# A windowed attention stage traced in a fixed order of TensorE instructions, with PSUM copies moved from VectorE to ScalarE

## The chip, the core and the metric

The kernel runs on one core of one Trainium2 chip. The metric is the device time of one execution in microseconds. A profile is one execution taken by the hardware profiler; its span runs from the first to the last instruction. Engines are named PE (TensorE matmul), PEld (TensorE weight load), DVE (VectorE), ACT (ScalarE), POOL (GpSimd) and SP (SyncE); a q after the name (SPq, ACTq) is the engine's queue of DMA issues.

## The reference

Attention with a causal window of 64 positions, then a gated feed-forward block. There are 8 batches and 8 heads, 576 positions, a head size of 64; the feed-forward block has 4608 tokens of 512 values and an inner size of 1536.

```python
scores = scale * np.matmul(q, k.transpose(0, 1, 3, 2))
mask = (rel >= 0) & (rel < window)          # window = 64, rel = row - column
scores = np.where(mask, scores, -1000000000.0)
... # softmax over the last axis
attn_out = np.matmul(attn, v)
x = attn_out.transpose(0, 2, 1, 3).reshape(B * S, H * D)
g = x @ w_gate
out = (g / (1 + np.exp(-g))) * (x @ w_val) @ w_out
```

## The kernel before

The kernel has two stages. The attention stage treats the 64 pairs of batch and head one after the other and fills xT, the attention's result with features on partitions, in bf16 in SBUF. The feed-forward stage then reads xT in nine tiles of 512 tokens. The change touches the attention stage alone.

A head is cut into nine blocks of 64 rows. Each block needs two blocks of keys (128 of them), and the blocks are worked in two groups, eight and one. The steps for a head, in the kernel's own words:

```python
nat = ...tile_pool(name="nat", bufs=2)      # q, k, v as loaded, and q_bf, k_bf
tp_pool = ...tile_pool(name="tps", bufs=2)  # qT, kT, v_aug, vs_aug
grp = ...tile_pool(name="grp", bufs=2)      # E, R, Dm, OU_sb
psA = ...(name="psA", bufs=2, space=PSUM)   # S_ps, OU, XT
psB = ...(name="psB", bufs=1, space=PSUM)   # tpq, tpk

# loads: q and v on SyncE's queue, k and the shifted v on ScalarE's
nc.sync.dma_start(q_nat[:, 0:4, :], ...)
nc.sync.dma_start(q_nat[0:64, 4, :], ...)
nc.scalar.dma_start(k_nat[:, 0:4, :], ...)
nc.scalar.dma_start(k_nat[0:64, 4, :], ...)
nc.sync.dma_start(v_nat[:, 0:4, :], ...)
nc.scalar.dma_start(vs_nat[:, :, :], ...)
# casts to bf16, then transposes through PSUM
nc.vector.tensor_copy(q_bf..., q_nat...)    # two, and two for k
for c in range(4):
    nc.tensor.transpose(tpq[:, 128*c:128*c+128], q_bf[:, c, :], identb[:])
    nc.tensor.transpose(tpk[:, 128*c:128*c+128], k_bf[:, c, :], identb[:])
nc.tensor.transpose(tpq[:, 512:576], ...)
nc.tensor.transpose(tpk[:, 512:576], ...)
nc.scalar.copy(qT[:, :], tpq[:, 0:576])
nc.vector.tensor_copy(kT[:, :], tpk[:, 0:576])
# v with a column of ones, so that OU's last column is the softmax sum
nc.vector.memset(...); nc.vector.memset(...)
nc.vector.tensor_copy(v_aug..., v_nat...); nc.vector.tensor_copy(vs_aug..., vs_nat...)
for gi, blocks in enumerate([list(range(8)), [8]]):
    for mu, i in enumerate(blocks):
        nc.tensor.matmul(S_ps[:, mu, :], kT[:, k0:k0+128], qT[:, 64*i:64*i+64])
    nc.scalar.activation(E, S_ps, AF.Exp, bias=0.0, scale=SCALE)
    nc.vector.tensor_mul(E, E, mask_t)
    for mu, i in enumerate(blocks):
        nc.tensor.matmul(OU[tt][:, jj, :], E[:, mu, :], vv)
    nc.vector.reciprocal(R, OU[tt][:, :, 64])            # one for each OU tile
    nc.vector.tensor_mul(Dm, ident8, R.to_broadcast(...))
    nc.vector.tensor_copy(OU_sb, OU[tt][:, :, 0:64])     # one for each OU tile
    for mu, i in enumerate(blocks):
        nc.tensor.matmul(XT[po:po+64, mu, :], OU_sb[:, mu, :], Dm[:, mu, :])
    nc.scalar.copy(xT[po:po+64, kc, ...], XT[po:po+64, ...])
```

The last matmul transposes a block and divides it by its softmax sum in one go: Dm is a diagonal matrix of reciprocals. The order in which the instructions of several heads are mixed on each engine is left to the scheduler. The weights are loaded first, 3 MB each for w_gate and w_out on SyncE's queue and for w_val on ScalarE's, and are cast to bf16 by VectorE.

The feed-forward stage makes, for each of 9 tiles and 12 slices of the inner size, four matmuls into g_ps and four into v_ps, a sigmoid on ScalarE and two products on VectorE; then 48 matmuls into o_ps, whose results go out through ScalarE.

Of the kernel before, what the change touches and what calls it, by code (L numbers as in the profile page):

```python
# [8 lines left out]
P = 128  # L9
FP32 = mybir.dt.float32  # L10
BF16 = mybir.dt.bfloat16
AF = mybir.ActivationFunctionType
# [4 lines left out]
def kernel(  # L17
# [10 lines left out]
    nc = tc.nc  # L28
    B, H, S, D = 8, 8, 576, 64
# [4 lines left out]
    SCALE = 1.0 / 8.0  # L34

    persist = ctx.enter_context(tc.tile_pool(name="persist", bufs=1))
    xT = persist.tile([P, 4, NTOK], BF16, name="xT")
# [14 lines left out]
    identb = persist.tile([P, P], BF16, name="identb")  # L52
    make_identity(nc, identb[:])
    ident8 = persist.tile([64, 8, 64], BF16, name="ident8")
# [22 lines left out]
    mask_reg = persist.tile([P, 8, 64], BF16, name="mask_reg")  # L77
    build_band(mask_reg[:], 8)
    mask_first = persist.tile([P, 8, 64], BF16, name="mask_first")
# [5 lines left out]
        base=0, pattern=[[1, 64]], channel_multiplier=-1,  # L85
    )

    with ExitStack() as actx:
        nat = actx.enter_context(tc.tile_pool(name="nat", bufs=2))
        tp_pool = actx.enter_context(tc.tile_pool(name="tps", bufs=2))  # L90
        grp = actx.enter_context(tc.tile_pool(name="grp", bufs=2))
        psA = actx.enter_context(tc.tile_pool(name="psA", bufs=2, space=bass.MemoryType.PSUM))
        psB = actx.enter_context(tc.tile_pool(name="psB", bufs=1, space=bass.MemoryType.PSUM))

        for b in range(B):
            for h in range(H):
                po = (h % 2) * 64
                kc = h // 2
                qbh = q[b, h]
                kbh = k[b, h]  # L100
                vbh = v[b, h]

                q_nat = nat.tile([P, 5, D], FP32, name="q_nat", tag="q_nat")
                k_nat = nat.tile([P, 5, D], FP32, name="k_nat", tag="k_nat")
                v_nat = nat.tile([P, 4, D], FP32, name="v_nat", tag="v_nat")
                vs_nat = nat.tile([P, 4, D], FP32, name="vs_nat", tag="vs_nat")
                nc.sync.dma_start(q_nat[:, 0:4, :], qbh[0:512].rearrange("(c p) d -> p c d", p=P))
                nc.sync.dma_start(q_nat[0:64, 4, :], qbh[512:576])
                nc.scalar.dma_start(k_nat[:, 0:4, :], kbh[0:512].rearrange("(c p) d -> p c d", p=P))
                nc.scalar.dma_start(k_nat[0:64, 4, :], kbh[512:576])  # L110
                nc.sync.dma_start(v_nat[:, 0:4, :], vbh[0:512].rearrange("(c p) d -> p c d", p=P))
                nc.scalar.dma_start(vs_nat[:, :, :], vbh[64:576].rearrange("(c p) d -> p c d", p=P))

                q_bf = nat.tile([P, 5, D], BF16, name="q_bf", tag="q_bf")
                k_bf = nat.tile([P, 5, D], BF16, name="k_bf", tag="k_bf")
                nc.vector.tensor_copy(q_bf[:, 0:4, :], q_nat[:, 0:4, :])  # L116
                nc.vector.tensor_copy(q_bf[0:64, 4, :], q_nat[0:64, 4, :])
                nc.vector.tensor_copy(k_bf[:, 0:4, :], k_nat[:, 0:4, :])  # L118
                nc.vector.tensor_copy(k_bf[0:64, 4, :], k_nat[0:64, 4, :])
                qT = tp_pool.tile([64, S], BF16, name="qT", tag="qT")  # L120
                kT = tp_pool.tile([64, S], BF16, name="kT", tag="kT")
                tpq = psB.tile([64, 640], BF16, name="tpq", tag="tpq")
                tpk = psB.tile([64, 640], BF16, name="tpk", tag="tpk")
                for c in range(4):
                    nc.tensor.transpose(tpq[:, 128 * c:128 * c + 128], q_bf[:, c, :], identb[:])  # L125
                    nc.tensor.transpose(tpk[:, 128 * c:128 * c + 128], k_bf[:, c, :], identb[:])  # L126
                nc.tensor.transpose(tpq[:, 512:576], q_bf[0:64, 4, :], identb[0:64, 0:64])  # L127
                nc.tensor.transpose(tpk[:, 512:576], k_bf[0:64, 4, :], identb[0:64, 0:64])
                nc.scalar.copy(qT[:, :], tpq[:, 0:576])  # L129
                nc.vector.tensor_copy(kT[:, :], tpk[:, 0:576])  # L130

                v_aug = tp_pool.tile([P, 5, 65], BF16, name="v_aug", tag="v_aug")
                vs_aug = tp_pool.tile([P, 4, 65], BF16, name="vs_aug", tag="vs_aug")
                nc.vector.memset(v_aug[:, :, 64:65], 1.0)
                nc.vector.memset(vs_aug[:, :, 64:65], 1.0)
                nc.vector.tensor_copy(v_aug[:, 0:4, 0:64], v_nat[:, 0:4, :])
                nc.vector.tensor_copy(vs_aug[:, :, 0:64], vs_nat[:, :, :])

                groups = [list(range(8)), [8]]
                for gi, blocks in enumerate(groups):  # L140
                    nb = len(blocks)
                    mask_t = mask_first if (gi == 0) else mask_reg
                    S_ps = psA.tile([P, 8, 64], FP32, name="S_ps", tag="S_ps")
                    for mu, i in enumerate(blocks):
                        k0 = 0 if i == 0 else 64 * (i - 1)
                        nc.tensor.matmul(  # L146
                            S_ps[:, mu, :],
                            kT[:, k0:k0 + 128],
                            qT[:, 64 * i:64 * i + 64],
                        )  # L150
                    E = grp.tile([P, 8, 64], BF16, name="E", tag="E")
                    nc.scalar.activation(  # L152
                        E[:, 0:nb, :], S_ps[:, 0:nb, :], AF.Exp, bias=0.0, scale=SCALE
                    )
                    nc.vector.tensor_mul(E[:, 0:nb, :], E[:, 0:nb, :], mask_t[:, 0:nb, :])  # L155

                    ntiles = 2 if nb == 8 else 1
                    OU = []
                    for tt in range(ntiles):
                        OU.append(psA.tile([64, 4, 65], FP32, name="OU", tag="OU"))  # L160
                    for mu, i in enumerate(blocks):
                        tt = mu // 4
                        jj = mu % 4
                        if i == 0:
                            vv = v_aug[:, 0, :]
                        elif i % 2 == 1:
                            vv = v_aug[:, (i - 1) // 2, :]
                        else:
                            vv = vs_aug[:, (i - 2) // 2, :]
                        nc.tensor.matmul(OU[tt][:, jj, :], E[:, mu, :], vv)  # L170
                    R = grp.tile([64, 8], FP32, name="R", tag="R")
                    for tt in range(ntiles):
                        nbt = min(4, nb - 4 * tt)
                        nc.vector.reciprocal(R[:, 4 * tt:4 * tt + nbt], OU[tt][:, 0:nbt, 64])
                    Dm = grp.tile([64, 8, 64], BF16, name="Dm", tag="Dm")
                    nc.vector.tensor_mul(  # L176
                        Dm[:, 0:nb, :],
                        ident8[:, 0:nb, :],
                        R[:, 0:nb].to_broadcast((64, nb, 64)),
                    )  # L180
                    OU_sb = grp.tile([64, 8, 64], BF16, name="OU_sb", tag="OU_sb")
                    for tt in range(ntiles):
                        nbt = min(4, nb - 4 * tt)
                        nc.vector.tensor_copy(  # L184
                            OU_sb[:, 4 * tt:4 * tt + nbt, :], OU[tt][:, 0:nbt, 0:64]
                        )
                    XT = psA.tile([P, 8, 64], FP32, name="XT", tag="XT")
                    for mu, i in enumerate(blocks):
                        nc.tensor.matmul(  # L189
                            XT[po:po + 64, mu, :],  # L190
                            OU_sb[:, mu, :],
                            Dm[:, mu, :],
                        )
                    i0 = blocks[0]
                    t0 = b * S + 64 * i0
                    nc.scalar.copy(  # L196
                        xT[po:po + 64, kc, t0:t0 + 64 * nb],
                        XT[po:po + 64, 0:nb, :],
                    )

    with ExitStack() as fctx:
        fps = fctx.enter_context(tc.tile_pool(name="fps", bufs=2, space=bass.MemoryType.PSUM))
# [70 lines left out]
```

The softmax here doesn't subtract the row's maximum and nothing guards it: scores larger than these inputs give would overflow.

## Time and profile before

| | |
|---|---|
| time, median of 6 runs | 605.72 us (605.02 to 606.32) |
| span of the profiled run | 604.6 us |
| PE busy | 519.7 us, 86% |
| DVE busy | 406.6 us, 67% |
| ACT busy | 218.3 us, 36% |
| first S_ps matmul, first g_ps matmul | 37.3 us, 316.6 us |
| bytes moved by DMA | 55.20 MB |

In a page of the profile, a row of instructions names line, engine, operation and tiles (out<-in), then the shape and the number of instructions, and after a bar the busy time in all and the mean of one in ns. In the timeline a row is the start in us, the time it took, the engine and the operation, and in brackets the idle time before it with the instruction that ended it. Where a row says x9 it merges nine instructions, and its time goes from the first one's start to the last one's end. Instructions of one engine are pipelined and overlap: the pace is read from start to start, and not from durations. The numbers such as 64*64 on a TensorE row are the rows and columns of the array that it uses. Busy shares are averages over stages that are bound by different things, so each stage is read by itself.

### The profile page before, as it was taken

How to read it: one execution, taken by the hardware profiler on the slowest of the kernel's cores; microseconds unless marked ns; L12 is line 12 of the kernel's file. 1: busy time of each engine (PE TensorE's matmuls, PEld its weight loads, DVE VectorE, ACT ScalarE, POOL GpSimd, SP SyncE). 2: the span in 40 equal slices, each digit the busy share in tenths (PEclk: the TensorE clock that was granted, in tenths of full speed). 3: DMA queues.
4: the chain of work that ended last, by engine and by line, in shares of the span. 5: the costliest groups of instructions: out<-in, count | busy, mean ns of one | idle time of the engine just before them, and what ended most of it. 6: DMA issues, size and time to landing. Idle time of an engine off the chain costs nothing. (4 is left out here: it accounts for less than half of the span.)

```text
span 604.6 us, 10370 instructions
## 1 busy us (share of the span) xinstructions
PE 519.7 (86%) x3664; PEld 306.4 (51%) x3664; DVE 406.6 (67%) x1439; ACT 218.3 (36%) x466; POOL 3.9 (1%) x12
## 2 busy tenths in 40 slices
PE   0068888888888888888869999999999999999996
PEld 0046666666666666666654444444444444444442
DVE  1578898898989889898966555454646363737280
ACT  0044444444444444445434233322333232323331
POOL 2000000000000000000000000000000000000000
PEclk9999999999999999999999999999999999999999
DMA  8954555555556555665510010101010101010101
GB/s 343 337 132 111 130 132 131 126 126 129 130 121 140 131 123 121 137 137 117 133 28 1 32 38 17 53 18 54 18 52 18 53 1 69 2 71 0 70 0 69
DMA packets 153251, 55.20 MB, mean 91 GB/s; under 512 B 146032, under 2 KB 146032, under 8 KB 153200
## 3 DMA queue, kind: packets, MB, share of 16 engines
q1 hardware_dynamic: 79968, 33.57, 20.1%
q10 hardware_dynamic: 73232, 20.98, 14.5%
q8 instruction: 28, 0.46, 0.4%
q14 instruction: 23, 0.19, 0.1%
HBM read 45.09 MB, written 9.44 MB: 90 GB/s over the span
## 5 line engine op out<-in xcount | busy, mean ns | idle before, releaser
L229 DVE TENSOR_TENSOR tq<-sg,g_ps 128x512 bf16<-128x512 bf16 x108 | 74.3, 688 | 82.1 <-ACT sg L227 82.1
L215 PE MATMUL g_ps<-xT,wg 128*128 128x512 bf16 x432 | 112.1, 382 | 0.7 <-ACT xT L196 0.7
L221 PE MATMUL v_ps<-xT,wv 128*128 128x512 bf16 x432 | 111.7, 381 | 0.0
L230 DVE TENSOR_TENSOR hT<-tq,v_ps 128x512 bf16<-128x512 bf16 x108 | 74.2, 687 | 43.5 <-PE v_ps L221 34.2
L227 ACT ACTIVATE sg<-g_ps 128x512 bf16<-128x512 f32 x108 | 64.5, 598 | 106.8 <-PE g_ps L215 106.7
L234 PE MATMUL o_ps<-wo,hT 128*128 128x512 bf16 x432 | 99.1, 379 | 2.0 <-ACT os__8323 L241 0.7
L152 ACT ACTIVATE E<-S_ps 128x512 bf16<-128x512 f32 (+1 forms) x128 | 46.8, 408 | 77.9 <-PE S_ps L146 51.5
L234 PEld LDWEIGHTS <-hT 128*128 128x128 bf16 x432 | 42.3, 98 | 53.5 <-issue 2.9
L215 PEld LDWEIGHTS <-wg 128*128 128x128 bf16 x432 | 42.5, 98 | 52.4 <-issue 2.3
L221 PEld LDWEIGHTS <-wv 128*128 128x128 bf16 x432 | 42.5, 98 | 51.6 <-issue 1.1
L126 PE MATMUL tpk<-identb,k_bf 128*64 128x128 bf16 x256 | 41.4, 313 | 30.8 <-DVE k_bf L118 25.5
L189 PE MATMUL XT<-Dm,OU_sb 64*64 64x64 bf16 x576 | 55.2, 240 | 14.5 <-DVE Dm L176 14.4
L184 DVE CAST OU_sb<-OU 64x256 bf16<-64x256 f32 (+1 forms) x192 | 63.4, 331 | 0.0
L196 ACT CAST xT<-XT 64x512 bf16<-64x512 f32 (+1 forms) x128 | 44.2, 394 | 47.9 <-PE XT L189 46.7
L170 PEld LDWEIGHTS <-E 128*64 128x64 bf16 x576 | 41.0, 151 | 31.2 <-DVE E L155 23.6
L176 DVE TENSOR_TENSOR Dm<-ident,R 64x512 bf16<-64x512 bf16 (+1 forms) x128 | 56.4, 441 | 0.0
L170 PE MATMUL OU<-v_aug,E 128*64 128x65 bf16 x320 | 41.5, 248 | 15.6 <-DVE E L155 13.1
L189 PEld LDWEIGHTS <-OU_sb 64*64 64x64 bf16 x576 | 41.8, 144 | 24.6 <-DVE Dm L176 15.9
L146 PE MATMUL S_ps<-qT,kT 64*128 64x64 bf16 x576 | 42.4, 237 | 12.7 <-DVE kT L130 10.9
L129 ACT COPY qT<-tpq 64x576 bf16<-64x576 bf16 x64 | 40.4, 631 | 27.7 <-PE tpq L127 21.1
L170 PE MATMUL OU<-vs_aug,E 128*64 128x65 bf16 x256 | 46.6, 249 | 0.7 <-DVE OU_sb L184 0.6
L125 PE MATMUL tpq<-identb,q_bf 128*64 128x128 bf16 x256 | 41.9, 311 | 4.1 <-DVE q_bf L116 2.8
(76 smaller groups left out, 377.6 us busy)
## 6 DMA issues: line engine op xcount, KB each, us to landing
k_nat<-in_k_dram ACTq DMA_DIRECT2D x64, 128.0 KB, 2.9
vs_nat<-in_v_dram ACTq DMA_DIRECT2D x64, 128.0 KB, 2.8
q_nat<-in_q_dram SPq DMA_DIRECT2D x64, 128.0 KB, 2.7
v_nat<-in_v_dram SPq DMA_DIRECT2D x64, 128.0 KB, 2.9
wv_f<-in_moe_w_val_dram ACTq DMA_DIRECT2D x1, 3072.0 KB, 18.0
wg_f<-in_moe_w_gate_dram SPq DMA_DIRECT2D x1, 3072.0 KB, 17.0
wo_f<-in_moe_w_out_dram SPq DMA_DIRECT2D x1, 3072.0 KB, 27.9
k_nat<-in_k_dram ACTq DMA_DIRECT2D x64, 16.0 KB, 2.5
```

The lines of the kernel that those rows point to most:

```text
L152: nc.scalar.activation(E[:, 0:nb, :], S_ps[:, 0:nb, :], AF.Exp, bias=0.0, scale=SCALE)
L170: nc.tensor.matmul(OU[tt][:, jj, :], E[:, mu, :], vv)
L176: nc.vector.tensor_mul(Dm[:, 0:nb, :], ident8[:, 0:nb, :], R[:, 0:nb].to_broadcast((64, nb, 64)),)
L184: nc.vector.tensor_copy(OU_sb[:, 4 * tt:4 * tt + nbt, :], OU[tt][:, 0:nbt, 0:64])
L189: nc.tensor.matmul(XT[po:po + 64, mu, :], OU_sb[:, mu, :], Dm[:, mu, :],)
L196: nc.scalar.copy(xT[po:po + 64, kc, t0:t0 + 64 * nb], XT[po:po + 64, 0:nb, :],)
L215: nc.tensor.matmul(g_ps[:], wg[:, kk, 128 * m:128 * m + 128], xT[:, kk, tok0:tok0 + 512], start=(kk == 0), stop=(kk == 3),)
L221: nc.tensor.matmul(v_ps[:], wv[:, kk, 128 * m:128 * m + 128], xT[:, kk, tok0:tok0 + 512], start=(kk == 0), stop=(kk == 3),)
L227: nc.scalar.activation(sg[:], g_ps[:], AF.Sigmoid)
L229: nc.vector.tensor_mul(tq[:], sg[:], g_ps[:])
L230: nc.vector.tensor_mul(hT[:, m, :], tq[:], v_ps[:])
L234: nc.tensor.matmul(o_ps[:], hT[:, kk, 128 * sub:128 * sub + 128], wo[:, kk, :], start=(kk == 0), stop=(kk == 11),)
```

## The change

The change rewrites the attention stage; what is computed stays the same. It has three parts.

First, the order. Every instruction of TensorE, VectorE and ScalarE in the stage is issued through a wrapper that keeps the order of the text on its engine, and the text is generated from a string. In it q and k are the 128-column transposes, Q and K the 64-column ones (after which the copy to qT or kT follows), S, O and X the matmuls into S_ps, OU and XT, D the loads of a head, Lq and Lk the casts, V the making of v_aug and vs_aug. One turn of the loop works on several heads: it loads head n+4, scores head n+1, casts head n+3, transposes head n+2, finishes block 8 of head n and starts OU of head n+1. It is meant to give TensorE work from other heads while VectorE and ScalarE work on one.

Second, who copies. The copy of kT out of PSUM and the two OU_sb copies of the group of eight go from VectorE to ScalarE.

Third, loads and buffers. All six loads of a head go through SyncE's queue, and the pools nat and grp have four buffers instead of two.

```diff
+    class Pinned:
+        """Every instruction issued through this keeps the order of the text on its engine."""
...
+    pe, dve, act = Pinned(nc.tensor), Pinned(nc.vector), Pinned(nc.scalar)
+    ORDER = (
+        "D4 Lq1 Lk1 V1 q4 Q1 k4 K1 Lq1 Lk1 S9 q4 Q1 k4 K1 Lq1 Lk1 O8 "
+        + "D1 V1 S9 Lq1 q4 Q1 k4 K1 O1 Lk1 X9 O8 " * 62
+        + "V1 S9 O1 X9 O9 X9"
+    )
-        nat = actx.enter_context(tc.tile_pool(name="nat", bufs=2))
+        nat = actx.enter_context(tc.tile_pool(name="nat", bufs=4))
...
-        grp = actx.enter_context(tc.tile_pool(name="grp", bufs=2))
+        grp = actx.enter_context(tc.tile_pool(name="grp", bufs=4))
...
-                nc.scalar.dma_start(k_nat[:, 0:4, :], kbh[0:512].rearrange("(c p) d -> p c d", p=P))
-                nc.scalar.dma_start(k_nat[0:64, 4, :], kbh[512:576])
+            nc.sync.dma_start(k_nat[:, 0:4, :], kbh[0:512].rearrange("(c p) d -> p c d", p=P))
+            nc.sync.dma_start(k_nat[0:64, 4, :], kbh[512:576])
...
-                nc.scalar.dma_start(vs_nat[:, :, :], vbh[64:576].rearrange("(c p) d -> p c d", p=P))
+            nc.sync.dma_start(vs_nat[:, :, :], vbh[64:576].rearrange("(c p) d -> p c d", p=P))
...
-                nc.vector.tensor_copy(kT[:, :], tpk[:, 0:576])
+            copy = act.copy if x == "q" else act.copy
+            copy(t[x + "T"][:, :], ps[:, 0:576])
...
-                        nc.vector.tensor_copy(
-                            OU_sb[:, 4 * tt:4 * tt + nbt, :], OU[tt][:, 0:nbt, 0:64]
-                        )
+                    copy = act.copy if g == 0 else dve.tensor_copy
+                    copy(OU_sb[:, 4 * tt:4 * tt + nbt, :], ous[tt][:, 0:nbt, 0:64])
...
```

For the ninth block (g == 1) VectorE makes R, Dm and OU_sb in that order.

More of the change, by code (lines that the diff above doesn't have):

```diff
@@ L86, with __init__, __getattr__ @@
     )
+    class Pinned:
+        def __init__(self, eng):
+            self.eng = eng
+        def __getattr__(self, name):
+            f = getattr(self.eng, name)
+            return lambda *a, **k: tc.keep_in_program_order(f(*a, **k))
+    pe, dve, act = Pinned(nc.tensor), Pinned(nc.vector), Pinned(nc.scalar)
[4 more added lines that the diff above has]
+    )
     with ExitStack() as actx:
-        nat = actx.enter_context(tc.tile_pool(name="nat", bufs=2))
+        nat = actx.enter_context(tc.tile_pool(name="nat", bufs=4))
@@ L90 @@
         tp_pool = actx.enter_context(tc.tile_pool(name="tps", bufs=2))
-        grp = actx.enter_context(tc.tile_pool(name="grp", bufs=2))
+        grp = actx.enter_context(tc.tile_pool(name="grp", bufs=4))
         psA = actx.enter_context(tc.tile_pool(name="psA", bufs=2, space=bass.MemoryType.PSUM))
         psB = actx.enter_context(tc.tile_pool(name="psB", bufs=1, space=bass.MemoryType.PSUM))
[L95 to L108, printed above, removed]
-                nc.scalar.dma_start(k_nat[:, 0:4, :], kbh[0:512].rearrange("(c p) d -> p c d", p=P))
-                nc.scalar.dma_start(k_nat[0:64, 4, :], kbh[512:576])
-                nc.sync.dma_start(v_nat[:, 0:4, :], vbh[0:512].rearrange("(c p) d -> p c d", p=P))
-                nc.scalar.dma_start(vs_nat[:, :, :], vbh[64:576].rearrange("(c p) d -> p c d", p=P))
[L114 to L149, printed above, removed]
-                        )
[L151 to L183, printed above, removed]
-                        nc.vector.tensor_copy(
-                            OU_sb[:, 4 * tt:4 * tt + nbt, :], OU[tt][:, 0:nbt, 0:64]
[L186 to L199, printed above, removed]
@@ new lines, with op_D @@
+        heads = [(b, h) for b in range(B) for h in range(H)]
+        st = {}
+        def op_D(n, i):
+            if n >= len(heads):
+                return
+            b, h = heads[n]
+            qbh, kbh, vbh = q[b, h], k[b, h], v[b, h]
+            t = st[n] = {}
+            q_nat = nat.tile([P, 5, D], FP32, name="q_nat", tag="q_nat")
+            k_nat = nat.tile([P, 5, D], FP32, name="k_nat", tag="k_nat")
+            v_nat = nat.tile([P, 4, D], FP32, name="v_nat", tag="v_nat")
+            vs_nat = nat.tile([P, 4, D], FP32, name="vs_nat", tag="vs_nat")
+            nc.sync.dma_start(q_nat[:, 0:4, :], qbh[0:512].rearrange("(c p) d -> p c d", p=P))
+            nc.sync.dma_start(q_nat[0:64, 4, :], qbh[512:576])
+            nc.sync.dma_start(k_nat[:, 0:4, :], kbh[0:512].rearrange("(c p) d -> p c d", p=P))
+            nc.sync.dma_start(k_nat[0:64, 4, :], kbh[512:576])
+            nc.sync.dma_start(v_nat[:, 0:4, :], vbh[0:512].rearrange("(c p) d -> p c d", p=P))
+            nc.sync.dma_start(vs_nat[:, :, :], vbh[64:576].rearrange("(c p) d -> p c d", p=P))
+            t["q_nat"], t["k_nat"] = q_nat, k_nat
+            t["v_nat"], t["vs_nat"] = v_nat, vs_nat
@@ new lines, in cast, with op_V @@
+        def cast(n, x):
+            if n >= len(heads):
+                return
+            t = st[n]
+            src = t[x + "_nat"]
+            bf = t[x + "_bf"] = nat.tile([P, 5, D], BF16, name=x + "_bf", tag=x + "_bf")
+            dve.tensor_copy(bf[:, 0:4, :], src[:, 0:4, :])
+            dve.tensor_copy(bf[0:64, 4, :], src[0:64, 4, :])
+        op_Lq = lambda n, i: cast(n, "q")
+        op_Lk = lambda n, i: cast(n, "k")
+        def op_V(n, i):
+            t = st[n]
+            t["v_aug"] = v_aug = tp_pool.tile([P, 5, 65], BF16, name="v_aug", tag="v_aug")
+            t["vs_aug"] = vs_aug = tp_pool.tile([P, 4, 65], BF16, name="vs_aug", tag="vs_aug")
+            dve.memset(v_aug[:, :, 64:65], 1.0)
+            dve.memset(vs_aug[:, :, 64:65], 1.0)
+            dve.tensor_copy(v_aug[:, 0:4, 0:64], t["v_nat"][:, 0:4, :])
+            dve.tensor_copy(vs_aug[:, :, 0:64], t["vs_nat"][:, :, :])
@@ new lines, with tp @@
+        LO = 0
+        def tp(n, x, c):
+            t = st[n]
+            if x + "ps" not in t:
+                t[x + "T"] = tp_pool.tile([64, S], BF16, name=x + "T", tag=x + "T")
+                t[x + "ps"] = psB.tile([64, 640], BF16, name="tp" + x, tag="tp" + x)
+            bf, ps = t[x + "_bf"], t[x + "ps"]
+            if c < 4:
+                return pe.transpose(ps[:, 128 * c:128 * c + 128], bf[:, c, :], identb[:])
+            r = pe.transpose(ps[:, 512:576], bf[0:64, 4, :], identb[0:64, 0:64])
+            copy = act.copy if x == "q" else act.copy
+            copy(t[x + "T"][:, :], ps[:, 0:576])
+            return r
@@ new lines, with op_S @@
+        op_q = lambda n, i: tp(n, "q", i)
+        op_k = lambda n, i: tp(n, "k", i)
+        op_Q = lambda n, i: tp(n, "q", 4)
+        op_K = lambda n, i: tp(n, "k", 4)
+        def op_S(n, i):
+            t = st[n]
+            if i in (0, 8):
+                t["S_ps"] = psA.tile([P, 8, 64], FP32, name="S_ps", tag="S_ps")
+            k0 = 0 if i == 0 else 64 * (i - 1)
+            mu = i % 8
+            S_ps = t["S_ps"]
+            r = pe.matmul(
+                S_ps[:, mu, :], t["kT"][LO:LO + 64, k0:k0 + 128], t["qT"][LO:LO + 64, 64 * i:64 * i + 64])
+            if i in (7, 8):
+                nb, g = (8, 0) if i == 7 else (1, 1)
+                mask_t = mask_first if g == 0 else mask_reg
+                E = t["E", g] = grp.tile([P, 8, 64], BF16, name="E", tag="E")
+                act.activation(E[:, 0:nb, :], S_ps[:, 0:nb, :], AF.Exp, bias=0.0, scale=SCALE)
+                dve.tensor_mul(E[:, 0:nb, :], E[:, 0:nb, :], mask_t[:, 0:nb, :])
+            return r
@@ new lines, in op_O @@
+        def op_O(n, i):
+            t = st[n]
+            g, mu = i // 8, i % 8
+            if i in (0, 4, 8):
+                t["OU", i // 4] = psA.tile([64, 4, 65], FP32, name="OU", tag="OU")
+            OU = t["OU", i // 4]
+            if i == 0:
+                vv = t["v_aug"][:, 0, :]
+            elif i % 2 == 1:
+                vv = t["v_aug"][:, (i - 1) // 2, :]
+            else:
+                vv = t["vs_aug"][:, (i - 2) // 2, :]
+            r = pe.matmul(OU[:, mu % 4, :], t["E", g][:, mu, :], vv)
+            if i in (7, 8):
+                nb, ntiles = (8, 2) if g == 0 else (1, 1)
+                ous = [t["OU", 0], t["OU", 1]] if g == 0 else [t["OU", 2]]
+                R = grp.tile([64, 8], FP32, name="R", tag="R")
+                for tt in range(ntiles):
+                    nbt = min(4, nb - 4 * tt)
+                    dve.reciprocal(R[:, 4 * tt:4 * tt + nbt], ous[tt][:, 0:nbt, 64])
+                Dm = t["Dm", g] = grp.tile([64, 8, 64], BF16, name="Dm", tag="Dm")
+                dve.tensor_mul(Dm[:, 0:nb, :], ident8[:, 0:nb, :], R[:, 0:nb].to_broadcast((64, nb, 64)))
+                OU_sb = t["OU_sb", g] = grp.tile([64, 8, 64], BF16, name="OU_sb", tag="OU_sb")
+                for tt in range(ntiles):
+                    nbt = min(4, nb - 4 * tt)
+                    copy = act.copy if g == 0 else dve.tensor_copy
+                    copy(OU_sb[:, 4 * tt:4 * tt + nbt, :], ous[tt][:, 0:nbt, 0:64])
+            return r
@@ new lines, in op_X @@
+        def op_X(n, i):
+            t = st[n]
+            b, h = heads[n]
+            po, kc = (h % 2) * 64, h // 2
+            g, mu = i // 8, i % 8
+            if i in (0, 8):
+                t["XT"] = psA.tile([P, 8, 64], FP32, name="XT", tag="XT")
+            XT = t["XT"]
+            r = pe.matmul(XT[po:po + 64, mu, :], t["OU_sb", g][:, mu, :], t["Dm", g][:, mu, :])
+            if i in (7, 8):
+                nb = 8 if g == 0 else 1
+                t0 = b * S + 512 * g
+                act.copy(xT[po:po + 64, kc, t0:t0 + 64 * nb], XT[po:po + 64, 0:nb, :])
+            return r
@@ new lines @@
+        ops = {"q": (op_q, 4), "Q": (op_Q, 1), "k": (op_k, 4), "K": (op_K, 1),
+               "S": (op_S, 9), "O": (op_O, 9), "X": (op_X, 9),
+               "D": (op_D, 1), "Lq": (op_Lq, 1), "Lk": (op_Lk, 1), "V": (op_V, 1)}
+        done = dict.fromkeys(ops, 0)
+        for token in ORDER.split():
+            name = token.rstrip("0123456789")
+            op, per = ops[name]
+            for _ in range(int(token[len(name):])):
+                op(*divmod(done[name], per))
+                done[name] += 1
```

## The prediction

> **What bounds the kernel now.** I read the busy digits of the 40 slices first, to see the stages.
>
> ```profile
> PE   0068888888888888888869999999999999999996
> DVE  1578898898989889898966555454646363737280
> ACT  0044444444444444445434233322333232323331
> ```
>
> One digit is 15.1 us. Slices 0 and 1 load the weights. Up to slice 20 (about 316 us) is attention, where neither TensorE nor VectorE is full. From slice 21 on TensorE is full: the feed-forward stage, which the change does not touch. In the timeline it starts at 316.61 us, so it takes 604.6 - 316.6 = 288.0 us, and I keep that. So the question is one number, the time of one head of attention, of which there are 64. Next I looked for a stretch that repeats, with the table by windows (columns: TensorE, weight loads, VectorE, ScalarE and so on, busy us and count).
>
> ```profile
> 60.00:86.20 26.20, 22.19 (x226) 16.78 (x225) 23.14 (x115) 12.20 (x31) 0.00 (x0) 1.00 0.57 129
> 86.20:112.40 26.20, 22.19 (x226) 16.78 (x225) 23.14 (x115) 12.21 (x31) 0.00 (x0) 1.00 0.58 130
> ```
>
> The two rows are the same, so 26.2 us is a period. Six heads fit in it: (316.6 - 37.3) / 64 = 4.36 us a head from the first S_ps matmul at 37.3 us. Per head VectorE works 23.14 / 6 = 3.86 us, TensorE 3.70 and ScalarE only 2.03. Who waits for whom, from 100 to 300 us (in all, times, longest):
>
> ```profile
> ACT E L152 <- PE S_ps L146: 35.8, 35, 2.1
> ...
> PEld L170 <- DVE E L155: 16.0, 31, 1.0
> DVE kT L130 <- PE tpk L128: 13.4, 23, 1.0
> ...
> PEld L189 <- DVE Dm L176: 10.8, 23, 0.5
> ...
> PEld L146 <- DVE kT L130: 10.1, 15, 0.7
> ```
>
> ScalarE starves (it costs nothing), while TensorE waits for VectorE for the mask, for Dm and for kT. VectorE is the busiest engine and the one waited for; the missing half microsecond per head is the two handing work to and fro. Last, the timeline, because I need start-to-start times (start, us, what):
>
> ```profile
> 201.22 0.66 PE L146 MATMUL S_ps<-qT,kT 64*128 64x64 bf16 x9
> ...
> 201.81 0.63 PE L125 MATMUL tpq<-identb,q_bf 128*64 128x128 bf16 x4
> ...
> 202.37 0.26 PE L127 MATMUL tpq<-identb,q_bf 64*64 64x64 bf16 x1
> ...
> 202.56 0.26 PE L170 MATMUL OU<-vs_aug,E 128*64 128x65 bf16 x1
> ...
> 202.86 0.16 DVE L174 RECIPROCAL R<-OU 64x1 f32<-64x1 f32 x1
> ...
> 203.07 0.21 DVE L176 TENSOR_TENSOR Dm<-ident,R 64x64 bf16<-64x64 bf16 x1
> ```
>
> ```profile
> 315.20 0.68 PE L189 MATMUL XT<-Dm,OU_sb 64*64 64x64 bf16 x9 [0.73 <-DVE Dm L176]
> ...
> 316.61 1.86 PE L215 MATMUL g_ps<-xT,wg 128*128 128x512 bf16 x4 [0.73 <-ACT xT L196]
> ...
> 325.52 1.03 PE L215 MATMUL g_ps<-xT,wg 128*128 128x512 bf16 x4
> ```
>
> The last two rows hold the TensorE clock: the same four matmuls take 1.86 us right after attention and 1.03 us later. So TensorE leaves attention at half rate, although the PEclk digits show 9 throughout. And the SyncE queue, one DMA issue after another:
>
> ```profile
> 30.20 0.58 SPq L111 DMA_DIRECT2D v_nat<-in_v_dram  x1
> 30.82 0.51 SPq L107 DMA_DIRECT2D q_nat<-in_q_dram  x1
> 31.40 0.53 SPq L108 DMA_DIRECT2D q_nat<-in_q_dram  x1
> ```
>
> That is 0.58 to 0.62 us from one issue to the next, 0.42 where the queue had been waiting.
>
> [...] in attention four 128-column transposes take 0.63 us with one at 0.31, 0.107 us apart[...]; full rate comes only some 4 us into the feed-forward stage. [...] 0.19 us from the 64*64 transpose at 202.37 to the 128*64 matmul at 202.56, against 0.055 us between matmuls of one mode (the XT row: (0.68 - 0.24) / 8). [...] The xT copies, 581 ns at 512 elements and 206 at 64, give 0.837 an element; so a 64x256 copy on ScalarE should take 206 + 192 x 0.837 = 367 ns, an estimate. [...] No run yet shows one queue alone in this stage.
>
> **Part 1: work moved from VectorE to ScalarE.** kT (449 ns) and two OU_sb copies of 397 ns leave VectorE. VectorE operations overlap by some 70 ns (kT starts at 199.80, the mask at 200.18), so this takes about 0.38 + 2 x 0.32 = 1.0 us from 3.86, leaving 2.9. ScalarE gets 631 (as the qT row) + 2 x 367 = 1.37 us, less 3 x 0.09 of overlap: 2.03 + 1.1 = 3.1 us. Both are then below what TensorE needs, so neither sets the pace by its sum.
>
> **Part 2: the fixed TensorE order.** I lay out one turn of the loop, S9 q4 Q1 k4 K1 O1 X9 O8, starting with S9 at 0, by the start-to-start times at half rate. S9 to q4: 0.59 (201.22 to 201.81). q4 to Q1: 0.56. Q1 to the next mode: 0.19. k4 the same 0.56, K1 0.19. So O1 starts at 0.59 + 0.56 + 0.19 + 0.56 + 0.19 = 2.09, and X9 at 2.28. Its last matmul could start at 2.28 + 8 x 0.055 = 2.72; then a switch of 0.19, and O8 to the next S9 takes 0.58 (200.64 to 201.22). Without waits: 2.72 + 0.19 + 0.58 = 3.49 us.
>
> The waits. The mask for O8: last S_ps of the first eight at 0.37, exp 0.27 later, mask 0.63 after that (312.09 to 312.72), O8 0.48 later: ready at 1.75, wanted at 2.9, hidden. kT for the next S9: K1 at 1.90, ScalarE copies from 2.2 to 2.83, wanted at 3.5 or later, hidden. Dm and OU_sb of the first eight are made in the turn before, hidden. One is not hidden: the ninth block. O1 is followed at once by X9, whose last matmul needs O1's own R, Dm and OU_sb. R starts 0.30 after OU (202.56 to 202.86), Dm 0.2 later, the OU_sb copy 0.13 after that, it lasts 0.2, and about 0.06 to TensorE: 0.89. X's ninth starts at 2.09 + 0.89 = 2.98, not 2.72. The turn is 2.98 + 0.19 + 0.58 = **3.75 us**.
>
> **Part 3: all loads on SyncE, four buffers.** Six issues a head at 0.58 to 0.60 are 3.5 to 3.6 us, just under 3.75. With four heads of lead this hides, but it is a floor: nothing gets below 3.5. The DMA engines, 57% busy at 4.36 us, would be 0.57 x 4.36 / 3.75 = 66% busy.
>
> **The sum.** Before the loop: wo lands at about 29.2 us (issued at 1.3, and 27.9 from issue to landing by the list of DMA issues), its cast (3.35) comes ahead of the first head's casts, so these start at 32.6, the transposes at 33.0, S9 of head 0 at 35.3 after the two copies on ScalarE, and the loop at about 38.2. Then 62 x 3.75 = 232.5, to 270.7. The tail (last S9, exp, mask, OU, Dm, XT, xT) I make 4.8; before it took 316.6 - 311.4 = 5.2. The feed-forward stage starts at 275.5 and ends at 563.5. The run times lie 1.1 above the span: **565 us**, 6.7% less.
>
> **Rivals.** (a) SyncE's queue or a single DMA ring becomes the bound. For: 3.5 to 3.6 against 3.75 is thin[...]. Against: issues after a wait take 0.42. At 0.67 us an issue the turn is 4.0 and the time 580; at 4.36 nothing would be won. (b) TensorE warms up. For: a denser stream. Against: attention never warmed up before, in 280 us with dense stretches. It would take 0.05 off each of eight transposes, 0.4 us; but then SyncE's 3.5 binds: 549. (c) The fixed order backfires: ScalarE, now 3.1 of 3.75 in strict order, delays exp behind the OU_sb copies, and the delay goes round. By my timetable the copies end some 0.05 us after the next exp could start, with a whole microsecond of slack behind it; if that is wrong by half a microsecond, 4.25 and 596. (d) The ninth block's wait is shorter than I think: 3.5, 549.
>
> **Range and chances.** Each 0.1 us of the turn is 6.2 us. The bounds 3.5 and 4.05 give 549 and 583. Within 2% needs a turn above 4.2, which takes (a) or (c) in a strong form: 5%. Slower needs more than 4.5 on every head, 1%.
>
> **What would show it.** Right: a period of about 3.75 us; TensorE's longest wait in it is XT for VectorE's OU_sb of the ninth block, about 0.26 a head; VectorE's busy share falls to about 75%, ScalarE's rises to 80%; four 128-column transposes still 0.63 us; first g_ps near 275. Wrong: TensorE or VectorE waiting for q_nat or v_nat (rival a),[...] S_ps waiting for E or kT (c), or a feed-forward stage that is not 288 us.

## The result, and the profile after

The changed kernel takes 566.02 us (median; 565.85 to 567.61) against 605.85 us for the kernel before in the same comparison: a ratio of 0.9351, 95% interval 0.9341 to 0.9362. The prediction was 565 us, in a range of 549 to 583. The profiled span is 564.1 us.

The busy digits of the page, 40 slices of 14.1 us each:

```profile
PE   0079999999999999999899999999999999999995
DVE  1578778778878777888483645637272736546370
ACT  0068878888878888888532323222332322232221
```

Counted from 0, attention now ends in slice 19, one earlier than before, and in attention TensorE shows 9 where it showed 8. ScalarE's digit went from 4 to 8: this is where VectorE's copies went.

The table by windows over ten turns of the loop (us; TensorE, weight loads, VectorE, ScalarE, GpSimd busy and count; clock, DMA share, GB/s):

```profile
100.00:137.60 37.60, 36.85 (x372) 27.97 (x373) 30.14 (x159) 31.98 (x81) 0.00 (x0) 1.00 0.66 148
```

VectorE is busy for 30.14 / 37.6 = 80% and ScalarE for 85%. These are the 75% and 80% of the prediction, each five points higher. (Its own sums, 2.9 and 3.1 us in a turn of 3.75, make 77% and 83%.) The DMA share is the predicted 66%.

The waits, from 80 to 260 us (in all, times, longest):

```profile
...
ACT OU_sb L95 <- DVE R L95: 16.7, 48, 1.6
PEld L95 <- DVE OU_sb L95: 12.2, 48, 1.2
...
DVE k_bf L95 <- DMA k_nat<-in_k_dram: 7.1, 11, 1.7
```

All three engines issue through one wrapper, so they share line 95, and the tiles tell the rows apart. What mattered before, TensorE waiting for the mask and for kT, has shrunk or gone. TensorE's largest wait is a weight load for VectorE's OU_sb, once a turn, 12.2 / 48 = 0.25 us. It is the ninth block, and the timeline shows it in one turn:

```profile
39.30 0.66 PE L95 MATMUL S_ps<-qT,kT 64*128 64x64 bf16 x9
...
41.40 0.26 PE L95 MATMUL OU<-vs_aug,E 128*64 128x65 bf16 x1
...
41.70 0.16 DVE L95 RECIPROCAL R<-OU 64x1 f32<-64x1 f32 x1 [0.23 <-PE OU L95]
41.89 0.22 DVE L95 TENSOR_TENSOR Dm<-ident,R 64x64 bf16<-64x64 bf16 x1
...
42.03 0.21 DVE L95 CAST OU_sb<-OU 64x64 bf16<-64x64 f32 x1
...
42.29 0.12 PEld L95 LDWEIGHTS <-OU_sb 64*64 64x64 bf16 x1 [0.21 <-DVE OU_sb L95]
...
43.06 0.66 PE L95 MATMUL S_ps<-qT,kT 64*128 64x64 bf16 x9
```

From S9 to S9 is 43.06 - 39.30 = 3.76 us. OU of block 8 starts at 41.40, VectorE makes R, Dm and OU_sb from it one after the other, and TensorE can load the copy at 42.29, 0.89 us after OU. ScalarE's wait for R, the first row shown of the waits, is no bound: TensorE hardly ever waits for the OU_sb that follows it (0.5 us in the whole span, by the page).

The end of attention, and SyncE's queue in the turn above:

```profile
276.31 1.86 PE L263 MATMUL g_ps<-xT,wg 128*128 128x512 bf16 x4 [0.64 <-ACT xT L95]
```

```profile
40.12 1.74 SPq L126 DMA_DIRECT2D q_nat<-in_q_dram  x1
41.90 0.51 SPq L127 DMA_DIRECT2D q_nat<-in_q_dram  x1
```

The first four g_ps matmuls still take 1.86 us, against 1.03 from 285.00 on, so TensorE still leaves attention at half rate. And one issue of the six took 1.74 us. Issues over 0.8 us are few, 17 of 284 from 60 to 240 us, but with them the mean is 0.566 us and 0.067 between two, so six cost 6 x 0.633 = 3.80 us: as much as a turn. By itself that sum proves nothing. A queue that is hardly ever idle (here 0.41 us at most between two issues) has the pace of the turn, whichever of the two leads; the runs below have to tell.

### The profile page after: what moved, and what is told of

Its sections match the earlier page's. It is cut to its first block, busy times and chain, and to the rows that moved or that the text cites. A ratio compares the mean times of both kernels' runs of the same rounds, so it can differ in the third digit from the quotient of the medians.

```text
span 564.1 us, 10318 instructions
## 1 busy us (share of the span) xinstructions
PE 518.1 (92%) x3664; PEld 306.3 (54%) x3664; DVE 353.6 (63%) x1247; ACT 292.1 (52%) x658; POOL 3.9 (1%) x12
## 4 chain that ended last, share of the span: by engine, by line
PE 76%; DMA 10%; DVE 9%; SPq 2%; issue 1%; ACT 1%; ACTq 0%
PE g_ps L263 17%; PE v_ps L269 17%; PE o_ps L282 17%; PE OU L95 7%; PE tpq L95 6%; PE tpk L95 6%; PE S_ps L95 5%; DMA wo_f<-in_moe_w_out_dram 5%; DMA q_nat<-in_q_dram 3%; DMA k_nat<-in_k_dram 3%; DVE Dm L95 3%; PE XT L95 2%; DVE R L95 2%; DVE OU_sb L95 1%; DVE E L95 1%
## 5 line engine op out<-in xcount | busy, mean ns | idle before, releaser
L95 PE MATMUL tpq<-identb,q_bf 128*64 128x128 bf16 (+1 forms) x320 | 52.6, 303 | 30.4 <-DVE q_bf L95 30.4
L95 PE MATMUL XT<-Dm,OU_sb 64*64 64x64 bf16 x576 | 56.8, 242 | 8.0 <-DVE OU_sb L95 3.2
L95 DVE TENSOR_TENSOR Dm<-ident,R 64x512 bf16<-64x512 bf16 (+1 forms) x128 | 57.6, 450 | 4.4
L95 PEld LDWEIGHTS <-q_bf 128*64 128x64 bf16 (+1 forms) x320 | 33.2, 151 | 46.9 <-DVE q_bf L95 30.4
L95 DVE RECIPROCAL R<-OU 64x4 f32<-64x4 f32 (+1 forms) x192 | 31.9, 168 | 34.9 <-PE OU L95 31.7
L95 PE MATMUL tpk<-identb,k_bf 128*64 128x128 bf16 (+1 forms) x320 | 52.7, 303 | 0.0
L95 ACT CAST OU_sb<-OU 64x256 bf16<-64x256 f32 x128 | 40.6, 366 | 21.0 <-DVE R L95 21.0
L95 PEld LDWEIGHTS <-OU_sb 64*64 64x64 bf16 x576 | 40.0, 146 | 21.2 <-DVE OU_sb L95 16.0
L95 ACT ACTIVATE E<-S_ps 128x512 bf16<-128x512 f32 (+1 forms) x128 | 45.3, 408 | 0.8 <-PE S_ps L95 0.7
## 6 DMA issues: line engine op xcount, KB each, us to landing
wo_f<-in_moe_w_out_dram SPq DMA_DIRECT2D x1, 3072.0 KB, 25.4
```

Source lines behind the costliest of these rows:

```text
L95: return lambda *a, **k: tc.keep_in_program_order(f(*a, **k))
```

## Experiments

Theory: TensorE's fixed order sets the turn of 3.76 us, with the ninth block's wait as its only wait. Rival: SyncE's queue of loads sets it, and the order only happens to be as long. A second question is what each of the three parts is worth by itself. Each ratio is to the kernel before.

### Take away the ninth block's wait

OU of block 8 moves ahead of the transposes, so that R, Dm and OU_sb are made behind them.

```diff
-        + "D1 V1 S9 Lq1 q4 Q1 k4 K1 O1 Lk1 X9 O8 " * 62
+        + "D1 V1 S9 O1 Lq1 q4 Q1 k4 K1 Lk1 X9 O8 " * 62
```

> The changed kernel with O1 (block 9 of OU) moved in the turn from just ahead of X9 to just behind S9, so that R, Dm and OU_sb of block 9 are made while TensorE transposes. Theory (the ninth block's wait bounds the turn): the wait of XT for OU_sb is gone, two changes of tiling mode fall away as well, and TensorE's own sum is about 3.2 us a turn; the queue of SyncE, six issues at 0.58 to 0.60 us, then becomes the bound: turn 3.5 to 3.6, time 548 to 555 us. Rival (SyncE's queue or the DMA already bounds the changed kernel): turn stays at 3.76, 563 to 567 us. Second rival (nothing behind TensorE binds): turn 3.25, about 532 us.

Measured: 563.09 us, ratio 0.9298 (0.928 to 0.9316); 3 us gained. Waits from 80 to 250 us:

```profile
PE OU L95 <- ACT OU_sb L95: 24.6, 35, 1.9
DVE k_bf L95 <- DMA k_nat<-in_k_dram: 23.7, 37, 2.0
```

The wait for VectorE's OU_sb is gone. In its place VectorE waits for k to arrive, in 37 places instead of 11, and the turns, 3.2 to 3.5 us where no load is late, average 3.72. (The first row is O1 waiting for a free OU buffer; with the loads relieved, two runs on, 7.1 us of it are left.) Six issues cost 6 x (0.554 + 0.068) = 3.73 us here. The rival's number held. That the queue of loads is the bound of this kernel, and stood level with the ninth block in the changed kernel, is a reading so far; the next two runs test it.

### Take two issues off SyncE's queue

In the changed kernel, GpSimd, which is idle in attention, issues the two small loads (the last 64 rows of q and of k).

```diff
-            nc.sync.dma_start(q_nat[0:64, 4, :], qbh[512:576])
+            nc.gpsimd.dma_start(q_nat[0:64, 4, :], qbh[512:576])
...
-            nc.sync.dma_start(k_nat[0:64, 4, :], kbh[512:576])
+            nc.gpsimd.dma_start(k_nat[0:64, 4, :], kbh[512:576])
```

> The changed kernel with the two small loads of a head (64 rows of q and of k) issued from GpSimd instead of SyncE: four issues a head on SyncE instead of six. Theory (TensorE's order with the ninth block's wait bounds the turn, and SyncE's queue only makes VectorE wait for k_nat now and then): these waits go, the mean turn falls from 3.79 to 3.76, 564 to 565 us. Rival (SyncE's issue rate of about 3.5 us a head is the real bound): turn towards 3.5, about 550 us.

Measured: 564.95 us, ratio 0.9332 (0.9317 to 0.9346). VectorE's waits for k_nat are gone and the turns of the loop are 3.76 us. With four issues the queue has time to spare: from 80 to 250 us it waits 45 times, 75.9 us in all, for a free v_nat buffer. This is the fixed order without disturbance: the mean turn of 3.79 in the changed kernel was 3.76 and some late loads.

### Both at once

The edits of the last two together.

> Both at once: O1 moved behind S9, and the two small loads of a head issued from GpSimd. Theory (with block 9 early SyncE's queue is the bound, 6 x 0.62 us = 3.73 measured; with four issues it needs 2.5): the turn falls to 3.25 us, set by ScalarE's line from kT over xT to OU_sb, for which O1 waits; about 532 us. Rival (not the issues but the DMA engines or the landing of k_nat hold it, 576 KB a head at some 158 GB/s): the turn stays near 3.7, 558 to 563 us.

Measured: 539.75 us, ratio 0.8913 (0.8897 to 0.8928), against 532 expected. (The 576 KB a head of the rival are 544 by the page.) The one gained 3 us, the other about 1 (its interval overlaps that of the changed kernel), both together 26: two limits of nearly the same length, and either hides the other. The turn is 3.20 and 3.49 us in alternation, 3.34 on average where 3.25 was expected, since a wait comes up in every second turn (80 to 250 us):

```profile
PE OU L95 <- ACT OU_sb L95: 7.1, 26, 0.5
```

O1 right behind S9 needs an OU buffer that ScalarE is still copying out.

### Block 8 in the middle, two ways

To avoid that wait, O1 goes behind the q transposes, with the small loads still on GpSimd.

```diff
-        + "D1 V1 S9 O1 Lq1 q4 Q1 k4 K1 Lk1 X9 O8 " * 62
+        + "D1 V1 S9 Lq1 q4 Q1 O1 k4 K1 Lk1 X9 O8 " * 62
```

> As the run before it, but with O1 between Q1 and k4 instead of behind S9, so that it comes after ScalarE has freed its OU buffer. Theory: O1 no longer waits, the turn is TensorE's own sum, about 3.2 us, 528 to 531 us. Rival (ScalarE, which works 2.9 us a head, sets the pace whatever TensorE's order): no difference to the run before it, within 1 us. In both: the transposes stay 0.107 us apart if TensorE's clock does not rise at this density[...].

Measured: 547.28 us, ratio 0.9038 (0.9022 to 0.9054), turn 3.47: both numbers missed, and worse than the kernel above. The text has VectorE cast q (Lq1) ahead of block 8's R, and the wait for OU_sb is back at 0.2 us a turn (80 to 240 us):

```profile
PEld L95 <- DVE OU_sb L95: 10.4, 46, 0.2
```

A place in TensorE's order is also a place in VectorE's. So the cast moves behind O1:

```diff
-        + "D1 V1 S9 Lq1 q4 Q1 O1 k4 K1 Lk1 X9 O8 " * 62
+        + "D1 V1 S9 q4 Q1 O1 Lq1 k4 K1 Lk1 X9 O8 " * 62
```

> As the run with block 9 in the middle and the small loads on GpSimd, but with the casts of q (Lq) behind O1 in the text, so that VectorE makes R, Dm and OU_sb of block 9 directly after the masks. In that run XT still waited 0.22 us a turn for OU_sb, since VectorE cast q first, and the turn was 3.47. Theory: without this wait 3.2 to 3.25 us, 531 to 535 us. Rival (ScalarE's line sets the pace as in the run with block 9 behind S9, 3.34 us in the mean): 538 to 541 us.

Measured: 538.56 us, ratio 0.889 (0.8877 to 0.8904), turn 3.32. The theory's 3.2 to 3.25 us was missed; the rival, ScalarE's own line, had the number. The table by windows over ten turns:

```profile
100.00:133.50 33.50, 33.08 (x377) 26.07 (x375) 30.03 (x161) 31.16 (x82) 10.57 (x21) 1.00 0.74 170
```

ScalarE is busy for 93%, TensorE for 99% by this table. From 80 to 250 us the mask waits for ScalarE's exp 25 times, in every second turn (6.5 us in all), and the weight load for block 8's OU_sb waits as often (6.4 us). That fits the rival; no run takes work off ScalarE to prove it. This kernel has the lowest median of the study, 538.56 / 566.02 = 0.951 of the changed kernel, though its interval overlaps that of both edits at once.

### Each part by itself

Copies back on VectorE, with order and loads as changed:

```diff
-            copy = act.copy if x == "q" else act.copy
+            copy = act.copy if x == "q" else dve.tensor_copy
...
-                    copy = act.copy if g == 0 else dve.tensor_copy
+                    copy = dve.tensor_copy
```

> The changed kernel with the copies of kT and OU_sb back on VectorE: order, loads and buffers of the change without its second part. Theory (VectorE at 3.86 us a head was the bound and has to be relieved, the order alone can't do it): VectorE's 4.0 us of work and its wait at the turn's end for OU give a turn of 4.4 to 4.5, 600 to 610 us, nothing won. Rival (the order alone does most of it): turn of 3.9 to 4.0, 572 to 580 us.

Measured: 609.76 us, ratio 1.0074 (1.0057 to 1.009), turn 4.48. As expected, XT waits for OU_sb late in VectorE's line, 0.8 us a head (80 to 250 us):

```profile
PE XT L95 <- DVE OU_sb L95: 30.3, 38, 0.8
```

The fixed order without the copies on ScalarE wins nothing.

Copies alone, in the kernel before, with its order left to the scheduler:

```diff
-                nc.vector.tensor_copy(kT[:, :], tpk[:, 0:576])
+                nc.scalar.copy(kT[:, :], tpk[:, 0:576])
...
-                        nc.vector.tensor_copy(
+                        (nc.scalar.copy if nb == 8 else nc.vector.tensor_copy)(
```

> The kernel before with only the copies of kT and of the group of eight's OU_sb moved to ScalarE: part two alone, in the scheduler's order. Theory (both parts are needed; the order leaves TensorE waiting for the chain of one head): VectorE falls to 2.9 us a head, some of TensorE's waits shrink, about 4.1 us a head, 585 to 595 us. Rival (VectorE's load is all): about 3.75 us a head, 565 to 570 us.

Measured: 631.28 us, ratio 1.0425 (1.041 to 1.0441), 4.80 us a head: slower, where theory and rival both had it faster. VectorE's busy time over the whole span fell from 406.6 to 348.6 us and a head still took longer, so less work on VectorE is not enough by itself. (The scheduler's order is another one here too: exp of one head starts 4.21 and 5.38 us after that of the head before, in turn.) Waits from 80 to 300 us:

```profile
PEld L170 <- DVE E L155: 33.2, 44, 0.8
...
PE OU L170 <- ACT OU_sb L184: 12.1, 23, 0.9
PE S_ps L146 <- ACT kT L130: 9.6, 22, 0.5
```

TensorE stands in the middle of a head and waits for that head's mask, its kT and its OU_sb. Which of the two copies is it? kT alone (the first two lines of the diff):

> The kernel before with only the copy of kT on ScalarE; OU_sb stays on VectorE, the scheduler keeps the order. Moving both cost 26 us, and this asks which did it. Theory (ScalarE is one line, in which kT now stands behind qT and xT, and S_ps waits for it): slower than before, 612 to 622 us. Rival (it is OU_sb, which on ScalarE must wait for R[...]): 590 to 603 us, VectorE relieved by 0.38 us a head.

Measured: 620.99 us, ratio 1.025 (1.0226 to 1.0275), the theory's time. ScalarE's kT copy takes 0.63 us and VectorE's 0.45, and S_ps waits for it in every second head (80 to 300 us):

```profile
PE S_ps L146 <- ACT kT L130: 16.5, 23, 0.7
```

That is 0.35 us a head, against 0.18 for VectorE's kT in the kernel before (8.2 us from 100 to 300 us), and a head grew by 0.24 us. But the scheduler's order changed as well: exp of a head now starts 3.25 and 6.12 us after that of the head before, in turn, where a pattern of six heads repeated before. So the loss is not shown to be this wait's alone. OU_sb alone (the last two lines):

> The kernel before with only the OU_sb copies of the group of eight on ScalarE; kT stays on VectorE. Theory (ScalarE's line and kT in it cost the time): near or under before, 590 to 608 us. Rival (the handing over from R on VectorE to OU_sb on ScalarE costs it): 615 us or more.

Measured: 630.62 us, ratio 1.041 (1.039 to 1.043). The theory fell and the time is the rival's, but the longest wait of TensorE is not the one that the rival names. Waits from 80 to 300 us:

```profile
PE OU L170 <- DVE E L155: 50.3, 46, 1.1
```

OU waits over a microsecond for the mask in every head. The scheduler chose another order for this kernel, in which nothing stands between a head's S_ps and its OU. How much of the loss is that order, and how much the slower handing on from ScalarE, these runs don't separate. The losses of the two, 15 and 25 us, also don't add up to the 26 of both.

Loads and buffers alone, in the kernel before:

```diff
-        nat = actx.enter_context(tc.tile_pool(name="nat", bufs=2))
+        nat = actx.enter_context(tc.tile_pool(name="nat", bufs=4))
...
-                nc.scalar.dma_start(k_nat[:, 0:4, :], kbh[0:512].rearrange("(c p) d -> p c d", p=P))
+                nc.sync.dma_start(k_nat[:, 0:4, :], kbh[0:512].rearrange("(c p) d -> p c d", p=P))
... (likewise grp, and the other two loads)
```

> The kernel before with only the third part: all six loads of a head on SyncE's queue, nat and grp with four buffers; the copies stay where they were and the scheduler keeps the order. Theory (loads were hidden before, and SyncE's 3.8 us for six issues fit into 4.38 us a head): no difference, 602 to 609 us. Rival (deeper buffers let the scheduler work further ahead and are worth something by themselves): 590 to 600 us. Second rival (one queue is too slow): above 612 us.

Measured: 607.49 us, ratio 1.0035 (1.0023 to 1.0047). Worth nothing alone: 2 us slower. Then the reverse: order, copies and buffers as changed, and the three loads back on ScalarE's queue.

```diff
-            nc.sync.dma_start(k_nat[:, 0:4, :], kbh[0:512].rearrange("(c p) d -> p c d", p=P))
-            nc.sync.dma_start(k_nat[0:64, 4, :], kbh[512:576])
+            nc.scalar.dma_start(k_nat[:, 0:4, :], kbh[0:512].rearrange("(c p) d -> p c d", p=P))
+            nc.scalar.dma_start(k_nat[0:64, 4, :], kbh[512:576])
... (likewise vs_nat)
```

> The changed kernel with k and the shifted v loaded from ScalarE's queue again, as before the change: order and copies without the third part's queue. Theory (an issue takes about 0.45 us of ScalarE's own line, in which the copies stand now; 2.9 + 3 x 0.45 = 4.25 us a head): about 594 us, 585 to 600. Rival (issues pass beside ScalarE's work and SyncE gets free): turn 3.76, 563 to 565 us.

Measured: 602.25 us, ratio 0.9934 (0.9911 to 0.9957), turn 4.32, a little above the theory's 585 to 600 us and 4.25. Nearly the whole gain is gone. ScalarE, its queue and the ninth XT matmul in one turn:

```profile
151.48 0.36 ACT L95 CAST OU_sb<-OU 64x256 bf16<-64x256 f32 x1 [0.41 <-DVE R L95]
151.65 0.47 ACTq L129 DMA_DIRECT2D k_nat<-in_k_dram  x1
151.75 0.37 ACT L95 CAST OU_sb<-OU 64x256 bf16<-64x256 f32 x1
152.16 0.60 ACTq L131 DMA_DIRECT2D vs_nat<-in_v_dram  x1
152.81 0.71 ACT L95 ACTIVATE E<-S_ps 128x512 bf16<-128x512 f32 x2 [0.69 <-PE tpq L95]
...
154.78 0.26 PE L95 MATMUL XT<-Dm,OU_sb 64*64 64x64 bf16 x1 [0.53 <-DVE OU_sb L95]
```

The exp starts 0.05 us after the issue of vs_nat ends, as in nearly every turn. S9 of this turn began at 151.33, so it comes 1.48 us after; in the changed kernel it came at 43.74 after S9 at 43.06, 0.68. The row puts the wait down to tpq, which exp does not read. What it stood behind is the issue, which is not counted as busy. The late exp makes the mask late, and VectorE then gets to block 8's R, Dm and OU_sb later: the ninth XT matmul starts 154.78 - 151.33 = 3.45 us after S9, where its weight load in the changed kernel started 42.29 - 39.30 = 2.99 after. That is the 0.46 us by which this turn, 4.22 us, is longer than 3.76; single turns are longer still.

Last, the order. The changed kernel with its own text, but without the keeping of the order:

```diff
-    pe, dve, act = Pinned(nc.tensor), Pinned(nc.vector), Pinned(nc.scalar)
+    pe, dve, act = nc.tensor, nc.vector, nc.scalar
```

> The changed kernel without the wrapper that keeps the order: text, copies, loads and buffers as changed, but the scheduler places the instructions. Theory (it is the fixed order, with other heads' matmuls between a head's steps, that makes the copies on ScalarE pay): 4.0 to 4.6 us a head, 580 to 615 us. Rival (the text, which traces four heads interleaved, and the buffers do it, keeping the order adds nothing): 560 to 570 us.

Measured: 661.64 us, ratio 1.093 (1.0912 to 1.0947), 5.36 us a head. The direction was right, the size far off: this is the slowest of all. Waits from 80 to 300 us:

```profile
DVE E L191 <- ACT E L190: 66.4, 41, 1.7
...
PE OU L206 <- DVE E L191: 40.1, 41, 1.1
```

It is the same chain, exp, mask, OU, run through with TensorE idle.

What the parts make together (us):

| order kept | copies on ScalarE | all loads on SyncE | time |
|---|---|---|---|
| no | no | no | 605.85 |
| no | yes | no | 631.28 |
| no | no | yes | 607.49 |
| no (new text) | yes | yes | 661.64 |
| yes | no | yes | 609.76 |
| yes | yes | no | 602.25 |
| yes | yes | yes | 566.02 |

The buffers are four wherever the loads are on SyncE or the order is kept. The order alone, with neither of the others, was not tried.

## Why the prediction was right

**The turn** was right, step by step. From S9 at 39.30, with the prediction's figure behind each: O1 at 2.10 (2.09), the first of X9 at 2.29 (2.28), the ninth at 2.99 (2.98), the next S9 at 3.76 (3.75). The ninth block's chain took the 0.89 us that was made up from four rows of the kernel before.

**What was to be hidden was hidden.** exp starts 43.74 - 43.06 = 0.68 us after S9. The prediction's own figures make that 0.37 + 0.27 and the 0.05 that the OU_sb copies hold it up, 0.69, and nothing waits for it. Rival (c), the fixed order backfiring, is absent here; the run with loads on ScalarE's queue shows how little it takes: 0.8 us more ahead of exp, and 0.56 us more a turn.

**The clock** stayed at half rate, against rival (b). Even at a turn of 3.32 us and with TensorE busy for 33.08 of 33.5 us by the table, four transposes take 0.63 us, as in the kernel before. In the feed-forward stage of the changed kernel four matmuls take 1.86 us at 276.31, 1.91 at 277.97, 1.16 at 279.68 and 1.03 at 280.67. What brings full rate there and not in attention these runs don't show, and that a denser stream would was the author's guess. The 0.05 us that rival (b) takes off a transpose is an estimate, about half of its 0.107, from the pace of these fours (1.66 us from start to start at 276.31, 0.86 at 285.00).

**The terms that were off** (us):

| term | predicted | measured | adds |
|---|---|---|---|
| first S9 of the loop | 38.2 | 35.54 | -2.7 |
| 62 turns | 62 x 3.75 = 232.5 | 270.75 - 35.54 = 235.2 | +2.7 |
| last S9 to first g_ps | 4.8 | 5.56 | +0.8 |
| feed-forward stage | 288.0 | 287.8 | -0.2 |
| median above span | 1.1 | 1.9 | +0.8 |

They sum to 1.4: the prediction's own sum was 564.6, rounded to 565, and the median is 566.0. The near hit of the total owes something to the first two, which cancel. The first: wo landed 25.4 us after its issue, and not 27.9. The second: 0.01 a turn is the start-to-start sum, and 0.03 is loads that come late, gone in the run with the small loads on GpSimd. The last is a misreading: 1.1 is the median of the kernel before less the span of an execution that itself took 606.32 us, 1.7 above its span; the changed kernel's profiled execution took 565.85, also 1.7 above. ScalarE's copies came as estimated: the 64x256 copy took 366 ns against 367, and two of them 0.64 us (at 43.21), which shows the prediction's overlap of 0.09.

**The step that was mis-sized** is "Six issues a head at 0.58 to 0.60 are 3.5 to 3.6 us, just under 3.75". They cost 3.73 to 3.80, because a few issues take up to 1.85 us. With it goes "With four heads of lead this hides": there was no lead. In the changed kernel k of a head lands 0.02 to 1.8 us before its cast (heads 6 to 63), and with two issues taken off the queue 5.8 to 8.8 us. Nor was it a full buffer that held the queue: the shifted v is issued 6.6 us or more after its buffer came free, against 0.3 with four issues. A floor at 3.75 instead of 3.5 changes the total little, but it makes rival (d) unreachable: a shorter ninth block was said to give 549 us, and gave 563 until two issues were taken off the queue. So rival (a) was level with the theory, and it is partly luck that the mean turn came out at 3.79 and not longer. Why single issues take so long stays open.

**What the prediction did not see** is that the parts depend on each other. It read part 3 as a cost alone, and with the loads back on two queues 36 of the 40 us are lost. It read part 1 as relief for VectorE, and in the scheduler's order the copies on ScalarE cost 26 us.

## What to carry to other kernels

Lay out one turn of a fixed order from start-to-start times, with every handing on as a step. Here that gave the turn to 0.01 us (3.75 against 3.76), but was short by 0.1 to 0.3 in the variants where ScalarE's or VectorE's own line came close (3.25 against 3.34, 3.2 against 3.47). Then do the same sum for each queue of DMA issues, on mean gaps with the long ones in. When two limits are of nearly the same length, removing one tells nothing about the other, so test them together. Before moving work to an idle engine, see whether that engine's line has room where the result is wanted. DMA issues stand in that line too (on ScalarE 0.37 to 0.60 us each), though its busy share does not show them.

## What the runs showed of the hardware that was not expected

- Issuing a load takes SyncE's queue 0.57 us on average with 0.07 between two, with single issues of 0.83 to 1.85 us; on ScalarE's queue in the kernel before it takes 0.37 to 0.60, with single ones up to 1.97. With three loads a head back on ScalarE's queue an exp starts 0.05 us after the issue ahead of it ends.
- Two loads of 16 KB a head cost GpSimd some 0.5 us each to issue (10.57 us for 21 in 33.5 us), and from 80 to 250 us no wait for them shows on TensorE, VectorE or ScalarE.
- With four of the six loads of a head on SyncE's queue and two on GpSimd's they kept up at 3.32 us a head, at a DMA share of 0.74 and 170 GB/s.
